# Attention scores of 18 tiles by matmuls over the full array with zeros in the moving rows, and one weight piece held behind its step

## The chip, the cores and the metric

The kernel runs as one program on one core of a Trainium2 chip. The metric is the device time of one launch in microseconds (us); lower is better. TensorE (PE, with its weight loads listed apart as PEld), VectorE (DVE), ScalarE (ACT) and GpSimd (POOL) each work through a queue of their own; SyncE (SP) issues most of the DMAs.

## The reference

Three layers follow each other, on 4 sequences of 768 tokens with 8 heads of 48 values (384 per token):

```python
# 1. linear attention with a decaying state, for each sequence and head
for t in range(768):
    cur = einsum('bhd,bhe->bhde', u * k_t, v_t)
    y[t] = einsum('bhd,bhde->bhe', r_t, state + cur)
    state = w * state + einsum('bhd,bhe->bhde', k_t, v_t)
# 2. x = y as [3072, 384];  h = x @ w_in (2048 wide);  x2 = (h - tanh(h)) @ w_out
# 3. top-1 mixture of 8 experts: the router normalizes x2 and the expert embeddings, divides by tau;
#    out[token] = gate * (relu(x2 @ w1[e]) @ w2[e])
```

## The kernel before

The 3072 tokens are 24 tiles of 128 (`NTILE`), three tiles to a block of 384 (`TOK`), eight blocks. A tile is one chunk of one sequence, and the chunks of a sequence are four tiles apart, so that the state of a sequence is handed on from tile n to tile n + 4.

**Attention of one tile** (class `Att`, tiles 6 to 23 by `attn_tile`). The transposed r and k of a tile (`RT`, `KT`) lie in 112 rows: four pairs of heads `q` along the columns, and within a pair the head g = 0 in rows 0 to 47 and g = 1 in rows 64 to 111, with zeros between. `decay_r` and `decay_k` multiply them in place by tables of decays (`tab_r`, `tab_k`) on POOL; `bonus`, `sums` and `diagonal` make the matrices `am`, which hold the u-term on their diagonal (POOL, DVE, POOL). `scores` (L423) makes for each pair q and head g the product of 128 keys by 128 queries: eight matmuls of 48 rows, those of g = 0 in the upper half of TensorE's rows and those of g = 1 in the lower half, into two PSUM banks `pa`. `causal` (L428) copies the scores under the diagonal into `am` on DVE. `values` (L454) multiplies `am` with v and the state with `RT` into `py`, in four column groups; `state` (L475, L484, L491) brings the state forward; `result` writes the sum into `xt` as a high and a low part. Each tile of `am` comes from a ring of four buffers, two for each tile of tokens.

**The first feed-forward layer** has 16 steps for each block. In step i `ffn1` (L557) makes 9 matmuls over 384 columns into `ph`; `squares` and `small_tanh` turn `ph` into a high part `ghi` (ACT, L625) and a low part `glo` (DVE, L635); `ffn2` (L572) uses those of three steps earlier (`LAG`) in 9 matmuls into three accumulators `acc`. While a block from 2 on goes through its steps, the attention of the block after it is emitted between them, three tiles in the first 12 steps.

**The experts.** In the last block (j = 7) the weights of the first expert are loaded in four pieces, in steps 8, 9, 13 and 15 (`load_expert`): a DMA brings a piece into one of two staging buffers `eraw` (so piece 2 waits until piece 0 is converted), ACT writes its high part in two halves (L885), and DVE and POOL write the low part of one half each (L886). The last piece stands under `tc.issue_after(mark["ghi"])`, which queues what it issues on ACT behind the latest `ghi`. The staging buffers then take pieces of the second expert.

**The order.** The start-up is ordered by hand. From there on a planner places every instruction into its engine's queue by modelled times and dependencies; the engines then work through their queues in order. A buffer that is written again makes the writer wait for its last readers.

Of the kernel before, what the change touches and what calls it, by code (L numbers as in the profile page):

```python
# [8 lines left out]
F32 = mybir.dt.float32  # L9
# [5 lines left out]
ALU = mybir.AluOpType  # L15
# [14 lines left out]
def rwkv__then__tanh_ffn__then__top1_moe_kernel(  # L30
# [14 lines left out]
    nc = tc.nc  # L45
    B = 4
    H, D = w.shape
# [3 lines left out]
    E, _, FF = w1.shape  # L51
    P = 128
    HP = H // 2
    NCH = S // P
    NK = DM // P
    TB = 3
# [15 lines left out]
    PW = 112  # L72
# [25 lines left out]
    work = ctx.enter_context(tc.tile_pool(name="work", bufs=2))  # L98
    dram = ctx.enter_context(tc.tile_pool(name="dram", bufs=1, space=DRAM))
    ps = ctx.enter_context(tc.tile_pool(name="ps", bufs=8, space=PSUM))  # L100
# [18 lines left out]
    def win(i, f, n=1):  # L119
        t = wq[i][f // 4].rearrange("p (f k d) -> p f k d", k=NK, d=P)  # L120
        return t[:, f % 4:f % 4 + n] if n > 1 else t[:, f % 4]
# [37 lines left out]
    ident = const.tile([P, P], F32, name="ident")  # L159
# [10 lines left out]
    cmask = const.tile([P, P], mybir.dt.uint8, name="cmask")  # L170
# [13 lines left out]
    tab_r = work.tile([PW, HP, P], F32, name="tab_r", bufs=1)  # L184
# [34 lines left out]
    mark = {}  # L219
# [62 lines left out]
    class Logits:  # L282


        def __init__(self, c, f):
            self.c, self.f = c, f
# [51 lines left out]
    def group(kk, g):  # L338
        return divmod((kk * P + 32 * g) // 32, 3)

    class Att:


# [51 lines left out]
        def sums(self):  # L395
            self.cd = work.tile([P, HP, 2], F32, name="cd")
            nc.vector.tensor_reduce(out=self.cd.rearrange("p a b -> p (a b)"), in_=self.rk, op=ALU.add, axis=AX.X)  # L397

        def diagonal(self, on_act=False, between=None):
            self.am = []  # L400
            for g in range(2):
                a = work.tile([P, HP, P], F32, name="am", bufs=4)
                if on_act:
                    for q in range(HP):
                        ins = nc.scalar.activation(out=a[:, q, :], in_=ident, func=AF.Copy,
                                                   scale=self.cd[:, q, g:g + 1]).ins
                    if between and g == 0:
                        with tc.issue_after(ins):
                            between()
                else:  # L410
                    nc.gpsimd.tensor_tensor(out=a, in0=ident[:, None, :].to_broadcast([P, HP, P]),  # L411
                                            in1=self.cd[:, :, g:g + 1].to_broadcast([P, HP, P]), op=ALU.mult)
                self.am.append(a)

        def scores(self, qs, idle=0):

            if qs[0] == 0:
                self.pa = [ps.tile([P, HP, P], F32, tag="p", name=f"pa{g}") for g in range(2)]
                fill(self.pa[0][:, :NK, :], idle)
            for q in qs:  # L420
                for g in range(2):
                    o = 64 * g
                    nc.tensor.matmul(out=self.pa[g][:, q, :], lhsT=self.KT[o:o + D, q, :], rhs=self.RT[o:o + D, q, :],  # L423
                                     start=True, stop=True)

        def causal(self):
            for g in range(2):
                nc.vector.copy_predicated(out=self.am[g], mask=cmask[:, None, :].to_broadcast([P, HP, P]),  # L428
                                          data=self.pa[g])
# [68 lines left out]
    def attn_tile(n):  # L498
        t = Att(n, None)
        with ExitStack() as es:  # L500
            for x in fence.pop(n, ()):
                es.enter_context(tc.issue_after(x))
            t.decay_r(nc.gpsimd)
            t.decay_k(nc.gpsimd)
            t.bonus(nc.gpsimd)
            t.sums()
            t.diagonal()
            t.decayed()
        yield
        t.scores(range(HP))  # L510
        t.causal()
        yield
        yield
        yield

        j = n // TB
        if j not in xts:
            xts[j] = work.tile([P, NK, 2, TOK], F32R, name="xt")
        t.xt = xts[j]
        t.values()  # L520
        t.state()
        t.result()
        yield
        yield
# [7 lines left out]
    def store_x(j, xt):  # L532
        with tc.issue_after(mark["w"]):
            nc.sync.dma_start(out=blocks(xd, j * TOK).rearrange("(p a) d -> p (a d)", p=P),
                              in_=xt.rearrange("p k i t -> p (k i t)").bitcast(F32))

    def attention(j):
        for n in range(TB * j, TB * j + TB):
            if 2 * TB + 1 < n + 1 < NTILE:
                load_rkv(n + 1)  # L540
            yield from attn_tile(n)


    def fill(bank, n):

        for _ in range(n):
            nc.tensor.matmul(out=bank, lhsT=ones16, rhs=ones16[:, None, :].to_broadcast([P, NK, P]), start=True,
                             stop=True)

    def ffn1(lhs, rhs, nk, n, idle=0, by_part=False):  # L550

        ph = ps.tile([P, n], F32, tag="p", name="ph")
        fill(ph, idle)
        turns = [(kk, p) for kk in range(nk) for p in range(3)]
        for kk, p in sorted(turns, key=lambda x: x[1]) if by_part else turns:
            a, b = ((0, 0), (0, 1), (1, 0))[p]
            mark["ph"] = nc.tensor.matmul(out=ph, lhsT=lhs[a][:, kk, :], rhs=rhs(b, kk),  # L557
                                          start=(kk == 0 and p == 0), stop=(kk == nk - 1 and p == 2)).ins
        return ph

    def columns_of(xt):
        return lambda p, kk: xt[:, kk, p, :]
# [46 lines left out]
    def squares(ph, between=None):  # L609
        z = work.tile([P, TOK], F32, name="z")  # L610
        q = work.tile([P, TOK], F32, name="q")
        nc.scalar.activation(out=z, in_=ph, func=AF.Square)  # L612
        if between:
            between()
        nc.scalar.activation(out=q, in_=z, func=AF.Square, scale=SS, bias=sb_t)  # L615
        return z, q

    def small_tanh(ph, parts, step, between=iter(())):

        z, q = parts  # L620
        ghi = work.tile([P, TOK], F32R, name="ghi", bufs=LAG + 1)
        glo = work.tile([P, TOK], F32R, name="glo", bufs=LAG + 1)
        nc.vector.tensor_tensor(out=ph, in0=ph, in1=z, op=ALU.mult)  # L623
        nc.vector.scalar_tensor_tensor(out=ph, in0=q, scalar=KC, in1=ph, op0=ALU.add, op1=ALU.mult)  # L624
        mark["ghi"] = nc.scalar.activation(out=ghi, in_=ph, func=AF.Copy).ins  # L625

        def outliers():
            mk = work.tile([P, TOK], BF16, name="mk", bufs=1)
            nc.scalar.activation(out=mk, in_=z, func=AF.Relu, bias=lz_t, accum_out=zx[:, step:step + 1])  # L629

        if step >= 2:
            outliers()
            for _ in range(3):
                next(between, None)
        mark["glo"] = nc.vector.tensor_tensor(out=glo, in0=ph, in1=ghi.bitcast(F32), op=ALU.subtract).ins  # L635
        if step < 2:
            late.append(outliers)
        return ghi, glo
# [807 lines left out]
    at = (-1, -1) + CONV  # L1446
    turns = {at[order.index(2 * c + 1)] + 1: c for c in range(NF // 2)}
    for i in range(len(steps) + 1):
        if i < len(steps):
            j, f = steps[i]  # L1450
# [85 lines left out]
    for j in (0, *range(2, NB)):  # L1536
        xt = xts.pop(j)
        store_x(j, xt)
        att = attention(j + 1) if 0 < j < NB - 1 else third
        na = 0 if j > 0 else 4  # L1540
        for n, i in enumerate(range(*spans[j])):
            ph = ffn1([win(p, i) for p in range(2)], columns_of(xt), NK, TOK)
            pend.append((j, i, small_tanh(ph, squares(ph), j * NF + i)))
            while na < ((n + 1) * 18 // NATT if j > 0 else 5 + 3 * n // 2):
                next(att, None)
                na += 1
            if len(pend) > LAG:
                ffn2_next()
            if n in FIN.get(j, FIN[NB]):
                next(fin, None)  # L1550
            if n in LIST.get(j, LIST[NB]):
                lists.pop(0)()
            if j == NB - 1 and i == 8:
                for _ in fin:
                    pass
                lists.pop(0)()
                order_first()
                places(0, 0, TB)
                sl = rows(0, 0, TB)
                gate = {}  # L1560
                ld = load_expert(0, sxi[0:1, 0, 1:2], gate, (nc.vector, nc.gpsimd))
                wides[0] = wide(0, sl)
            if j == NB - 1 and i in (8, 9, 13, 15):
                with tc.issue_after(mark["ghi"]) if i == 15 else ExitStack():
                    next(ld, None)
            if j == NB - 1 and i in COL0:
                next(wides[0])
        for _ in att:
            pass
# [92 lines left out]
```

## Time and profile before

| | us |
|---|---|
| runs | 769.98, 771.24, 769.98 (median 769.98) |
| the profiled execution | 771.22, of which the span of its instructions is 769.6 |
| PE busy | 756.2 (98% of the span), 6143 matmul records |
| PEld, DVE, ACT, POOL busy | 718.4, 464.8, 457.1, 300.5 |

A busy share says how much of the span an engine had work in hand; matmuls overlap in a pipeline, so what a matmul costs is read from the distance between starts, not from its own duration. A matmul of plain float32 operands stands in the trace as two records, one of `float32r` or bfloat16 as one.

### The profile page before, as it was taken

Reading aid. Unit: us, or ns where it says so; the run is one execution under the profiler, and the core shown is the slowest. Engines: PE = TensorE matmul, PEld = TensorE weight load, DVE = VectorE, ACT = ScalarE, POOL = GpSimd, SP = SyncE. Lnnn points to the kernel's source line nnn. Section 1 sums busy time; section 2 is a strip of 40 time slices with the busy share of each in tenths; the row PEclk is TensorE's granted clock in tenths of the full one; section 3 lists DMA queues with packets and bytes.
Section 4 is the critical chain, followed back from the end, with each engine's and each line's share of the span. In section 5 each row is a group of like instructions: output and inputs, shape, how many; then the busy total and the mean of one; then the engine's idle time right before and its main releaser. Section 6 shows DMA issues by size and latency. Waiting matters only on the chain.

```text
span 769.6 us, 15995 instructions
## 1 busy us (share of the span) xinstructions
PE 756.2 (98%) x6143; PEld 718.4 (93%) x6143; DVE 464.8 (60%) x1037; ACT 457.1 (59%) x1064; POOL 300.5 (39%) x362
## 2 busy tenths in 40 slices
PE   9899999999999999999999999999999999999996
PEld 5689899999999999999999999999989999999996
DVE  7967976667656565565555655656684455545430
ACT  5787676655657556656657756768463535544431
POOL 3743680466781671753564341133530202110111
PEclk9899999999999999999999999999999999999999
DMA  8964355243240330232223101052374435454400
GB/s 263 288 206 142 118 170 200 64 165 100 66 148 24 126 122 2 91 94 87 80 69 123 59 32 64 14 171 85 116 229 143 129 115 189 150 173 161 154 31 32
DMA packets 41016, 92.21 MB, mean 120 GB/s; under 512 B 4827, under 2 KB 20597, under 8 KB 39907
## 3 DMA queue, kind: packets, MB, share of 16 engines
q1 hardware_dynamic: 36274, 81.44, 33.0%
q0 software_dynamic: 4240, 9.67, 3.5%
q8 instruction: 50, 0.82, 0.4%
q14 instruction: 36, 0.29, 0.1%
q10 hardware_dynamic: 416, 0.00, 0.0%
HBM read 67.26 MB, written 24.00 MB: 119 GB/s over the span
## 4 chain that ended last, share of the span: by engine, by line
PE 90%; issue 3%; DVE 3%; ACT 2%; DMA 2%; POOL 1%; POOLq 0%; SPq 0%; DVEq 0%; ACTq 0%
PE acc L572 39%; PE ph L557 37%; PE py L454 5%; PE pa L423 3%; DMA eraw<-in_moe_w_dram 2%; PE pt L908 1%; PE warm L158 1%; PE pst L475 1%; POOL out_dram L827 0%; PE pt L293 0%; DVE bits L267 0%; DVE wraw L270 0%; PE pl L303 0%; DVE bits L264 0%; PE accn L1036 0%
## 5 line engine op out<-in xcount | busy, mean ns | idle before, releaser
L557 PE MATMUL ph<-xt,wq 128*128 128x384 f32 (+4 forms) x1712 | 340.1, 341 | 1.9 <-ACT wt L295 1.3
L557 PEld LDWEIGHTS ph<-xt,wq 128*128 128x128 f32 x1712 | 302.7, 188 | 5.9 <-ACT wt L295 1.5
L572 PE MATMUL acc<-wq,ghi 128*128 128x392 f32 (+2 forms) x1120 | 289.1, 343 | 0.9 <-ACT ghi L625 0.9
L572 PEld LDWEIGHTS acc<-wq,ghi 128*128 128x128 f32 (+1 forms) x1120 | 200.3, 187 | 5.9 <-ACT ghi L625 1.2
L572 PE MATMUL acc<-wq,glo 128*128 128x392 f32 (+2 forms) x552 | 182.2, 340 | 0.1
L612 ACT ACTIVATE z<-ph 128x384 f32<-128x384 f32 x128 | 62.8, 490 | 105.0 <-PE ph L557 104.7
L623 DVE TENSOR_TENSOR ph<-ph,z 128x384 f32<-128x384 f32 x128 | 72.0, 563 | 62.6 <-ACT z L612 62.0
L572 PEld LDWEIGHTS acc<-wq,glo 128*128 128x128 f32 (+1 forms) x552 | 102.7, 187 | 0.9 <-DVE glo L635 0.7
L635 DVE TENSOR_TENSOR glo<-ph,ghi 128x384 fp32r<-128x384 f32 x128 | 70.7, 553 | 45.7 <-ACT ghi L625 45.6
L827 POOL DMA_INDIRECT out_dram<-ob,gts x27 | 27.2, 1008 | 176.6 <-ACT ob L917 171.4
L625 ACT ACTIVATE ghi<-ph 128x384 fp32r<-128x384 f32 x128 | 62.6, 490 | 41.0 <-DVE ph L624 37.6
L615 ACT ACTIVATE q<-z,sb_t 128x384 f32<-128x384 f32 x128 | 78.9, 617 | 3.4
L624 DVE SCALAR_TENSOR_TENSOR ph<-q,ph 128x384 f32<-128x384 f32 x128 | 71.7, 560 | 12.5 <-ACT q L615 3.5
L629 ACT ACTIVATE mk<-z,lz_t 128x384 bf16<-128x384 f32 x128 | 77.1, 603 | 0.0
L653 DVE SCALAR_TENSOR_TENSOR glo<-ph,ghi 128x384 fp32r<-128x384 f32 (+2 forms) x56 | 30.7, 549 | 63.8 <-ACT ghi L651 63.8
L651 ACT ACTIVATE ghi<-ph 128x384 fp32r<-128x384 f32 (+4 forms) x56 | 27.5, 491 | 67.6 <-PE ph L557 67.5
L411 POOL TENSOR_TENSOR am<-ident,cd 128x512 f32<-128x512 f32 x36 | 36.8, 1045 | 77.8 <-DVE cd L397 77.1
L886 DVE TENSOR_TENSOR wq<-eraw,wq 128x768 fp32r<-128x768 f32 x60 | 55.1, 955 | 11.5 <-ACT wq L885 11.0
L885 ACT ACTIVATE wq<-eraw 128x768 fp32r<-128x768 f32 x64 | 50.4, 839 | 6.2 <-DMA eraw<-in_moe_w_dram 6.2
L278 POOL TENSOR_TENSOR wq<-wraw,wq 128x768 fp32r<-128x768 f32 (+1 forms) x17 | 30.3, 1782 | 39.6 <-ACT wq L277 38.5
L716 POOL DMA_INDIRECT tab<-tk,irow x24 | 24.4, 1019 | 31.8 <-DVE tk L744 25.1
L491 POOL TENSOR_TENSOR st<-st,pw 112x384 f32<-112x384 f32 x20 | 16.7, 840 | 49.2 <-DVE st L484 43.7
(287 smaller groups left out, 860.0 us busy)
## 6 DMA issues: line engine op xcount, KB each, us to landing
eraw<-in_moe_w_dram SPq DMA_DIRECT2D x32, 768.0 KB, 4.5
rkv<-in_rows_dram SPq DMA_DIRECT2D x18, 640.0 KB, 5.6
tt<-in_cols_dram SPq DMA_DIRECT2D x22, 448.0 KB, 4.4
xd<-xt SPq DMA_DIRECT2D x8, 1152.0 KB, 8.0
wraw<-in_moe_w_in_dram SPq DMA_DIRECT2D x8, 768.0 KB, 8.6
wraw<-in_moe_w_out_dram SPq DMA_DIRECT2D x8, 768.0 KB, 5.2
rkv<-xe SPq DMA_DIRECT2D x22, 192.0 KB, 4.4
xe<-zero SPq DMA_DIRECT2D x2, 1536.0 KB, 15.4
```

Source lines behind the costliest of these rows:

```text
L454: nc.tensor.matmul(out=self.py[32 * g:32 * g + 32, kk, :], lhsT=lhs, rhs=rhs, start=start, stop=stop)
L557: mark["ph"] = nc.tensor.matmul(out=ph, lhsT=lhs[a][:, kk, :], rhs=rhs(b, kk), start=(kk == 0 and p == 0), stop=(kk == nk - 1 and p == 2)).ins
L572: mm = nc.tensor.matmul(out=acc[t][:lhs.shape[1]], lhsT=lhs, rhs=rhs(b, i), start=(i == span[0] and p == 0), stop=(i == span[1] - 1 and p ...
L612: nc.scalar.activation(out=z, in_=ph, func=AF.Square)
L615: nc.scalar.activation(out=q, in_=z, func=AF.Square, scale=SS, bias=sb_t)
L623: nc.vector.tensor_tensor(out=ph, in0=ph, in1=z, op=ALU.mult)
L624: nc.vector.scalar_tensor_tensor(out=ph, in0=q, scalar=KC, in1=ph, op0=ALU.add, op1=ALU.mult)
L625: mark["ghi"] = nc.scalar.activation(out=ghi, in_=ph, func=AF.Copy).ins
L629: nc.scalar.activation(out=mk, in_=z, func=AF.Relu, bias=lz_t, accum_out=zx[:, step:step + 1])
L635: mark["glo"] = nc.vector.tensor_tensor(out=glo, in0=ph, in1=ghi.bitcast(F32), op=ALU.subtract).ins
L885: nc.scalar.activation(out=hi[c][:, a], in_=t[:, a], func=AF.Copy)
L886: engs[s % len(engs)].tensor_tensor(out=lo[c][:, a], in0=t[:, a], in1=hi[c][:, a].bitcast(F32), op=ALU.subtract)
```

## The change

From tile 6 on, a method `masked` runs first in a tile: four DVE multiplications, each of 48 rows by two pairs of 128 columns, write r times its decay table into two tiles `rtm`, in which a pair q has 256 columns: the first 128 hold head g = 0 in rows 0 to 47, the last 128 hold head g = 1 in rows 64 to 111, and all other rows are zero from one memset at the beginning. `scores` then makes four matmuls of 112 rows by 256 columns, one for each pair, in place of eight of 48 rows by 128 columns. `RT` itself is still multiplied by the table on POOL, for `values`. The scores and the diagonals are grouped by pairs of heads instead of by row half, and `mixed`, which takes the place of `am`, is one pair of tiles for all 18 tiles, as `rtm` is: the ring of four `am` buffers is taken by these four for good.

In the last block, piece 2 of the first expert's weights (step 13) is put behind its step's `ghi` on ACT, as piece 3 already was.

```diff
@@ in the kernel's body
+    fixed = []
+
+    class Pairs:
+        def __init__(self, tiles, g):
+            self.tiles, self.g = tiles, g
+
+        def __getitem__(self, at):
+            return self.tiles[at[1] // 2][:, at[1] % 2, self.g, :]
@@ class Att
+        def masked(self, eng):
+            if not fixed:
+                fixed.extend(work.tile([P, 2, 2, P], F32, name="am", bufs=4) for _ in range(4))
+                for x in fixed[2:]:
+                    nc.gpsimd.memset(x, 0.0)
+            self.mixed, self.rtm = fixed[:2], fixed[2:]
+            for i in range(2):
+                for g in range(2):
+                    o = slice(64 * g, 64 * g + D)
+                    eng.tensor_tensor(out=self.rtm[i][o, :, g, :], in0=self.RT[o, 2 * i:2 * i + 2],
+                                      in1=tab_r[o, 2 * i:2 * i + 2], op=ALU.mult)
+
         def diagonal(self, on_act=False, between=None):
+            if self.n >= 2 * TB:
+                self.am = [Pairs(self.mixed, g) for g in range(2)]
+                for i in range(2):
+                    nc.gpsimd.tensor_tensor(out=self.mixed[i].rearrange("p q g t -> p (q g) t"),
+                                            in0=ident[:, None, :].to_broadcast([P, 4, P]),
+                                            in1=self.cd[:, 2 * i:2 * i + 2, :].rearrange("p q g -> p (q g)")[:, :, None]
+                                            .to_broadcast([P, 4, P]), op=ALU.mult)
+                return
@@ scores
+            if self.n >= 2 * TB:
+                self.pa = [ps.tile([P, 2, 2, P], F32, tag="p", name=f"pa{i}") for i in range(2)]
+                for q in qs:
+                    nc.tensor.matmul(out=self.pa[q // 2][:, q % 2], lhsT=self.KT[:, q, :], rhs=self.rtm[q // 2][:PW, q % 2],
+                                     start=True, stop=True)
+                return
@@ causal
+            if self.n >= 2 * TB:
+                for i in range(2):
+                    nc.vector.copy_predicated(out=self.mixed[i].rearrange("p q g t -> p (q g) t"),
+                                              mask=cmask[:, None, :].to_broadcast([P, HP, P]),
+                                              data=self.pa[i].rearrange("p q g t -> p (q g) t"))
+                return
@@ attn_tile
+            t.masked(nc.vector)
             t.decay_r(nc.gpsimd)
@@ steps of the last block
-                with tc.issue_after(mark["ghi"]) if i == 15 else ExitStack():
+                with tc.issue_after(mark["ghi"]) if i >= 13 else ExitStack():
                     next(ld, None)
```

## Rows read from the trace of the kernel before

**Rows 1.** The page: busy time, and the chain that ended last, by engine.

```profile
PE 756.2 (98%) x6143; PEld 718.4 (93%) x6143; DVE 464.8 (60%) x1037; ACT 457.1 (59%) x1064; POOL 300.5 (39%) x362
...
PE 90%; issue 3%; DVE 3%; ACT 2%; DMA 2%; POOL 1%; POOLq 0%; SPq 0%; DVEq 0%; ACTq 0%
```

**Rows 2.** Waits of PE: us in total, times, longest.

```profile
PE acc L572 <- ACT ghi L625: 0.9, 1, 0.9
```

**Rows 3.** Timeline of PE, two steps: start, us, instruction, count, idle before.

```profile
451.23 1.75 PE L557 MATMUL ph<-xt,wq 128*128 128x384 f32 x9
...
454.44 1.75 PE L557 MATMUL ph<-xt,wq 128*128 128x384 f32 x9
456.12 1.16 PE L423 MATMUL pa<-tt 48*128 48x128 f32 x16
...
458.94 1.75 PE L557 MATMUL ph<-xt,wq 128*128 128x384 f32 x9
```

**Rows 4.** Groups of PE by shape, 120 to 470 us: busy us, mean ns, idle.

```profile
L423 PE MATMUL pa<-tt 48*128 48x128 f32 x288 | 20.9, 285 | 0.0
L475 PE MATMUL pst<-rkv,ktok 128*16 128x48 f32 x224 | 7.2, 206 | 0.0
L454 PE MATMUL py<-am,rkv 128*32 128x128 f32 x576 | 27.1, 272 | 0.0
```

**Rows 5.** Timeline of PE around 135 us, one state product.

```profile
134.94 0.52 PE L475 MATMUL pst<-rkv,ktok 128*32 128x48 f32 x32
```

**Rows 6.** Timeline of PE around 527 us, transposes over the whole array.

```profile
526.77 1.14 PE L908 MATMUL pt<-ident,rkv 128*128 128x128 f32 x9
527.67 0.60 PE L572 MATMUL acc<-wq,ghi 128*128 128x392 f32 x2
528.12 0.34 PE L572 MATMUL acc<-wq,glo 128*128 128x392 f32 x1
```

**Rows 7.** Groups of DVE by shape, 520 to 640 us: busy us, mean ns, idle.

```profile
L912 DVE TENSOR_TENSOR xt<-pt,xt 128x256 fp32r<-128x256 f32 x6 | 2.5, 417 | 1.5 <-ACT xt L910 1.5
```

**Rows 8.** Windows, one block: us, busy of PE, PEld, DVE, ACT, POOL, then granted clock.

```profile
244.00:306.00 62.00, 62.00 (x612) 59.76 (x611) 37.16 (x83) 38.56 (x96) 32.73 (x37) 1.00 0.25 84
```

**Rows 9.** Timeline of POOL: diagonals of tile 8, decay of r of tile 9.

```profile
147.04 2.05 POOL L411 TENSOR_TENSOR am<-ident,cd 128x512 f32<-128x512 f32 x2 [2.11 <-DVE cd L397]
...
156.52 1.29 POOL L355 TENSOR_TENSOR tt<-tt,tab_r 112x512 f32<-112x512 f32 x1 [1.24 <-DMA tt<-in_cols_dram]
```

**Rows 10.** Timeline of PE: state product of tile 7, scores of tiles 8 and 9.

```profile
152.25 0.52 PE L475 MATMUL pst<-rkv,ktok 128*32 128x48 f32 x32
...
156.96 1.16 PE L423 MATMUL pa<-tt 48*128 48x128 f32 x16
...
176.42 1.16 PE L423 MATMUL pa<-tt 48*128 48x128 f32 x16
```

**Rows 11.** Timeline of DVE: the causal copies of tile 8.

```profile
158.73 1.37 DVE L428 COPY_PREDICATED am<-cmask,pa 128x512 f32<-128x512 uint8 x2
```

**Rows 12.** Timeline of ACT in the last block, 520 to 555 us.

```profile
520.23 0.84 ACT L885 ACTIVATE wq<-eraw 128x768 fp32r<-128x768 f32 x1 [1.08 <-DMA eraw<-in_moe_w_dram]
520.98 0.47 ACT L625 ACTIVATE ghi<-ph 128x384 fp32r<-128x384 f32 x1
...
522.46 0.83 ACT L885 ACTIVATE wq<-eraw 128x768 fp32r<-128x768 f32 x1
...
532.75 0.49 ACT L625 ACTIVATE ghi<-ph 128x384 fp32r<-128x384 f32 x1 [0.39 <-DVE ph L624]
...
554.21 1.57 ACT L885 ACTIVATE wq<-eraw 128x768 fp32r<-128x768 f32 x2
```

**Rows 13.** Timeline of PE in the last block, steps 12 and 13.

```profile
518.85 1.75 PE L557 MATMUL ph<-xt,wq 128*128 128x384 f32 x9
521.51 0.98 PE L572 MATMUL acc<-wq,ghi 128*128 128x392 f32 x4 [0.91 <-ACT ghi L625]
...
523.58 1.74 PE L557 MATMUL ph<-xt,wq 128*128 128x384 f32 x9
```

**Rows 14.** Timeline of SP: loads of the second expert's first two pieces.

```profile
525.26 14.48 SPq L859 DMA_DIRECT2D eraw<-in_moe_w_dram  x2
```

## The prediction

> **What bounds the kernel now.** I read the page first, then the waits of PE, then PE's timeline step by step. The page shows PE busy for 98% of the span and 90% of the chain that ended last on PE [rows 1]. A busy PE is not proof that it sets the time, so the waits come next: once the start-up is over, the only entry of any size in which PE waits for another engine is one wait of 0.9 us for a high part in the last block [rows 2]. The timeline then shows what a step costs. One without attention goes from one start of `ph` to the next in 454.44 − 451.23 = 3.21 us; the following one, with the scores of a tile in it, in 458.94 − 454.44 = 4.50 us [rows 3]. So the scores of a tile cost 1.29 us of PE's queue, and with PE as the bound every such microsecond stands in the total. In a block with attention DVE is busy for 37 of 62 us, ACT for 39 and POOL for 33, at a granted clock of 1.00, TensorE's upper level of 2.4 GHz [rows 8]. What the change does to those three counts only where it makes PE wait.
>
> **The scores, before.** A tile's eight matmuls are 16 records of 128 columns; the 18 tiles make the 288 records of the group, busy for 20.9 us, 1.16 us a tile as in the one shown [rows 3, 4]. The price of 1.29 us holds two things. The records run in pairs, upper and lower half of the rows side by side, and stream for 8 times the price of 128 columns. That price is about 0.109 us: nine transposes of 128 columns over the whole array take 1.14 us, the last one's own 0.27 us left out, for eight distances [rows 6]. So some 0.87 us are streaming, and 0.42 us are lost around it, going into the halves and out of them. Such a loss does not belong to plain float32 over the whole array: from the first of those transposes to the third `acc` matmul behind them are 1.35 us, which nine distances of 0.109 and two of the usual 0.18 us (3.21 us over 18 matmuls) fill, 1.34 us [rows 3, 6].
>
> The Trainium skill says the same of the cause: the page TensorEngine Tiling (Array Packing), section Key Properties, has it that a change of the tiling mode drains TensorE. If that drain were all that changes, the 18 tiles would win 18 × 0.42 = 7.6 us; the trace agrees on the drain, but not on the rest of the sum.
>
> **The scores, after.** There are eight records of 256 columns a tile, one after the other. What does a record's column cost? The records of 48 columns last 206 ns, those of 128 columns 272 ns: 66 ns for 80 columns, 0.825 ns a column, two cycles of 2.4 GHz [rows 4]. Ends are modelled in these records, so I want a distance as well: the state product puts 32 records of 48 columns, four side by side, into 0.52 us, so (0.52 − 0.21) / 7 = 0.044 us for each four, against 0.109 us for 128 columns, with weights of only 16 and 32 columns [rows 5, 6]. It is the moving columns that set the pace, not the loading of weights. A record of 256 columns then costs between 256 × 0.825 = 0.211 us and twice 0.109 = 0.218 us. I take 0.215: eight make 1.72 us. The zeros are streamed at full price. A tile costs 1.72 − 1.29 = 0.43 us more, 18 tiles **7.7 us** (bounds 18 × 0.40 = 7.2 and 18 × 0.45 = 8.1).
>
> **The new DVE work.** Four multiplications of 256 elements a row: a DVE operation of that size took 417 ns, so 1.67 us a tile and 30 us in all [rows 7]. In the block of the windows it raises DVE by 5 us, to 42 of 62 us [rows 8]; a `glo` is used three steps, 9.6 us, after its `ph`. I take nothing, with all 1.67 us of each tile as the bound from above, which would ask for every one of them to lie ahead of something that PE awaits. The two memsets on POOL happen once.
>
> **The shared tiles.** With one pair `rtm` for all tiles, `masked` of tile 9 can only write once the scores of tile 8 have read, at 158.1 us; it must stand before the in-place decay of r, which POOL now starts at 156.52 us [rows 9, 10]. That decay moves back to about 160 us, and with it what is queued behind it on POOL (the bonus, the diagonals, the keys' decay if the planner leaves it there). Its first readers, the scores of tile 9, come at 176.42 us [rows 10], so 16 us cover it. With one pair `mixed`, the diagonals of tile 8 (147.04 us) can't be written before the values of tile 7 are done, about 152.3 us, when the state product has begun [rows 9, 10]. They would end at 154.4 us, 4.3 us before the causal copies of tile 8 at 158.73 us [rows 11]. Nothing here reaches PE, if the planner, which knows these dependencies, queues them so. If the cover were gone, the causal copies and then the values would be late. Grouping the diagonals and the causal copies by pairs changes neither their number nor their size.
>
> **The weight piece.** Steps 12 and 13 start 523.58 − 518.85 = 4.73 us apart instead of 3.21: 1.52 us lost, 0.91 us of it as one idle stretch that `ghi` ended [rows 13]. The cause stands on ACT: it waited 1.08 us for the DMA of piece 2, converted half of it (0.84 us), and only then came to the `ghi` that PE wanted, at 520.98 us; the second half stands at 522.46 us [rows 12]. The `ghi` of step 13 is four such parts later. With the piece behind it, ACT has 1.08 us of waiting and 1.67 us of copies less in front of PE's need, more than the 1.52 us. They return as 1.67 us on ACT in steps 13 and 14, where ACT had caught up: it stood idle for 0.39 us before a `ghi` at 532.75 us, and would be there up to 2.75 us earlier [rows 12]. Two things queue behind: the low parts on DVE and POOL, needed by the first expert's second product after the block, and the load of the second expert's first piece on SP, which issued at 525.26 us as the staging buffer came free, and would move to about 530 us; its conversion is at 554.21 us [rows 12, 14]. I take **−1.5 us**; the bounds are 0 (the wait comes back with another instruction) and −1.8 (0.2 us more in the step before).
>
> **The sum.** 771.22 us of the profiled execution + 7.7 − 1.5 = 777.4 us. The median of the runs, 769.98, lies 1.24 us under that execution, so the time should be 776.2 us. By the bounds, 775.4 to 778.1.
>
> **The rivals.**
> 1. *Faster: the halves' drain was the price, and wide records are cheap.* If a record's pace were set by loading its 128 columns of weights, 0.109 us, 256 moving columns would hide behind it: 8 × 0.109 = 0.87 us, 0.42 us less a tile, 7.6 us in all, 769.98 − 7.6 − 1.5 = 760.9 us. It decides once a record of 256 columns takes under 1.29 / 8 = 0.161 us. For it speaks that 128 columns of weights and 128 moving columns are equally dear in the transposes; against it the pace of the 48-column records, whose weights are short and whose cost still goes with the moving columns [rows 4, 5]. 7%.
> 2. *The shared tiles or the new DVE work make PE wait.* A chain from values through diagonals and causal copies to the next values, tile by tile, has 4.3 us to spare where I looked; if the planner spends it, or DVE's 1.67 us stand before a `causal` that PE awaits, 0.2 to 0.4 us a tile give 3.6 to 7.2 us more: 779.8 to 783.4 us. PE's row of waits speaks against it [rows 2]. 10%.
> 3. *The piece's wait only moves.* Then only the scores count: 777.7 us. 10%.
> 4. *The wide scores pay the drain too,* 0.42 us a tile: 783.8 us. The transposes speak against it [rows 6]. 2%.
> 5. *The planner, whose whole order is made anew, gives the 6 us back by chance.* There is no idle time of PE for that beyond the stall already counted [rows 2]: 5%, about 770 us.
>
> **How the numbers follow.** The forecast has 66%, and its own range is 774.5 to 778.5 us with an order made anew. To leave out no more than two in ten, the range takes in the third rival and the lower end of the second: 773.5 to 781 us. About 0.2%, 1.5 us, is what a measurement tells from no change. Slower: the forecast and rivals 2 to 4, 88%; the same: rival 5, 5%; faster: rival 1, 7%.
>
> **What would show it.** Right: eight records of 112 rows by 256 columns a tile, about 0.215 us apart and some 380 ns long, steps with scores at about 4.9 us instead of 4.50, no lengthened matmuls at either end; PE without the wait for `ghi` near 521 us, the copies of piece 2 behind the `ghi` of step 13. Wrong: records 0.11 us apart, or waits of PE for `am`, `pa` or `glo` in the blocks with attention, or DVE standing before `masked` while a `ph` waits.

## The result, and the profile after

| | before | after |
|---|---|---|
| median of the runs, us | 770.44 (769.98 to 771.24, 4 runs) | 782.23 (780.48 to 782.94, 4 runs) |
| the profiled execution, us | 771.22 | 782.94, span 781.3 |

The ratio is 1.0149 (95% interval 1.0129 to 1.0168): 11.8 us slower. The forecast was 776.2 us with a range of 773.5 to 781.0. The sign was right, the forecast change of +6.2 us is little more than half of the measured one, and the time lies 1.2 us above the range.

Where the 11.8 us stand is read by laying the two timelines of PE over each other: the start of the same `ph` in both kernels, after less before. Each flat stretch costs nothing, each rise is a loss at a known place. (Below, steps are counted through all blocks: in before step 12 starts at 93.07 us, step 24 at 138.68, step 40 at 204.44, the experts at 538.93.)

| stretch (time in after) | the shift of `ph` goes from, to | us | what lies in it |
|---|---|---|---|
| to 93 us | 0 to 0.26 | +0.26 | the start-up |
| 93 to 145 us | 0.26 to 6.04 | +5.78 | the scores of one tile (0.44) and **5.34 of something else** |
| 145 to 481 us | 6.04 to 13.58 | +7.54 | the scores of 17 tiles, 0.44 each |
| 519 to 551 us | 13.58 to 11.78 | −1.80 | the weight piece |

Two of the three terms came as forecast; a third, of 5.3 us at one place, was not in the sum. First the forecast ones. This is the timeline of PE in after, the two steps that answer to [rows 3]:

```profile
464.36 1.75 PE L602 MATMUL ph<-xt,wq 128*128 128x384 f32 x9
...
467.58 1.75 PE L602 MATMUL ph<-xt,wq 128*128 128x384 f32 x9
469.16 1.89 PE L452 MATMUL pa<-am,tt 112*128 112x256 f32 x8
...
472.52 1.75 PE L602 MATMUL ph<-xt,wq 128*128 128x384 f32 x9
```

The step without scores takes 467.58 − 464.36 = 3.22 us as before, the step with them 472.52 − 467.58 = 4.94 us instead of 4.50: +0.44 us. The group of these records by their tile (count, then shortest, median and longest duration in ns) shows their length:

```profile
L452 PE MATMUL pa<-am,tt x144: 377/379/382, 128.7 to 470.7; 112*128 112x256 f32 x144
```

All 144 last within 5 ns of each other, none is lengthened at an end, and what the step has over one without scores, 4.94 − 3.22 = 1.72 us, is eight times 0.215 us with nothing left over. So nothing is lost around the wide records, and the zeros are streamed at full price.

The weight piece is seen on ACT and on PE in the last block of after, where [rows 12] and [rows 13] were read before:

```profile
539.73 0.48 ACT L670 ACTIVATE ghi<-ph 128x384 fp32r<-128x384 f32 x1
540.10 1.58 ACT L930 ACTIVATE wq<-eraw 128x768 fp32r<-128x768 f32 x2
```

```profile
528.99 1.75 PE L602 MATMUL ph<-xt,wq 128*128 128x384 f32 x9
...
532.17 1.75 PE L602 MATMUL ph<-xt,wq 128*128 128x384 f32 x9
...
535.37 1.39 PE L602 MATMUL ph<-xt,wq 128*128 128x384 f32 x7
```

Both halves of piece 2 now stand behind the step's `ghi`, and the steps that were 4.73 us apart are 535.37 − 532.17 = 3.20 us apart.

Now the 5.3 us. The waits of PE in after (us in total, times, longest) begin with an entry that before does not have; the `ghi` entry is a wait of 0.55 us at 120.5 us, no longer the one of the last block:

```profile
PE pt L293 <- DVE wq L313: 2.7, 1, 2.7
...
PE acc L617 <- ACT ghi L670: 0.6, 1, 0.6
```

In the timeline of PE that wait, in brackets, stands at 97 us. The later `ph` and transposes behind it are slow:

```profile
96.70 0.34 PE L617 MATMUL acc<-wq,glo 128*128 128x392 f32 x1
99.74 0.62 PE L293 MATMUL pt<-ident,wraw 128*128 128x128 f32 x3 [2.71 <-DVE wq L313]
100.12 1.97 PE L617 MATMUL acc<-wq,ghi 128*128 128x392 f32 x6
101.88 0.84 PE L293 MATMUL pt<-ident,wraw 128*128 128x128 f32 x3
102.38 2.54 PE L602 MATMUL ph<-xt,wq 128*128 128x384 f32 x9
104.75 0.69 PE L617 MATMUL acc<-wq,glo 128*128 128x392 f32 x3
```

PE waits for a conversion on DVE (`wq`, L313, 0.17 us long). Why that came late shows in the timeline of DVE; the conversion is the last line. First the same instruction in before, then the timeline of after:

```profile
93.50 0.16 DVE L313 TENSOR_TENSOR wq<-pw__1363,wq 128x16 fp32r<-128x16 f32 x1
```

```profile
89.72 0.42 DVE L267 SCALAR_TENSOR_TENSOR bits<-wraw,bits 128x256 int32<-128x256 int32 x1
90.22 5.16 DVE L420 TENSOR_TENSOR am<-tt,tab_r 48x256 f32<-48x256 f32 x2
95.41 0.69 DVE L264 TENSOR_SCALAR bits<-wraw 128x512 int32<-128x512 int32 x1
96.01 0.56 DVE L668 TENSOR_TENSOR ph<-ph,z 128x384 f32<-128x384 f32 x1
96.60 0.90 DVE L420 TENSOR_TENSOR am<-tt,tab_r 48x256 f32<-48x256 f32 x1
...
97.86 0.42 DVE L420 TENSOR_TENSOR am<-tt,tab_r 48x256 f32<-48x256 f32 x1
...
99.51 0.17 DVE L313 TENSOR_TENSOR wq<-pw__1363,wq 128x16 fp32r<-128x16 f32 x1
```

L420 is the new `masked` (its tiles `rtm` bear the name `am` in the trace). Two of its operations together take 5.16 us: the first the usual 0.42 us, the second, from 90.66 us on, **4.72 us**. The timeline of POOL over the same stretch gives the reason:

```profile
89.66 0.99 POOL L415 MEMSET am<- 128x512 f32 x2
90.62 1.29 POOL L369 TENSOR_TENSOR tt<-tt,tab_k 112x512 f32<-112x512 f32 x1
91.87 1.01 POOL L403 TENSOR_TENSOR rk<-rkv 128x384 f32<-128x384 f32 x1
92.83 1.01 POOL L399 TENSOR_TENSOR ktok<-rkv,ktab 128x384 f32<-128x384 f32 x1
93.81 1.28 POOL L369 TENSOR_TENSOR tt<-tt,tab_k 112x512 f32<-112x512 f32 x1
95.05 1.20 POOL L399 TENSOR_TENSOR ktok<-rkv,ktab 128x384 f32<-128x384 f32 x1
96.22 1.00 POOL L404 TENSOR_TENSOR rk<-rk,u_bc 128x384 f32<-128x384 f32 x1
```

From 90.62 us on POOL runs operation after operation with no gap. The DVE operation that was started beside it ends at 95.38 us, 0.29 us after the fourth of them; the one of 0.90 us that starts at 96.60 us ends at 97.50 us, 0.28 us after the operation that POOL had in hand. The first one, of 0.42 us, ran beside a memset, which reads nothing.

The stall costs twice. These are windows of after (length, busy time of PE, PEld, DVE, ACT and POOL with counts, then the granted clock):

```profile
92.00:96.00 4.00, 4.00 (x26) 4.00 (x25) 3.97 (x2) 0.36 (x3) 4.00 (x4) 1.00 0.00 0
96.00:100.00 4.00, 1.29 (x8) 0.97 (x7) 3.87 (x10) 1.76 (x4) 2.86 (x4) 1.00 0.00 0
100.00:104.00 4.00, 4.00 (x17) 3.89 (x17) 4.00 (x11) 3.11 (x8) 2.27 (x2) 0.57 0.00 0
104.00:108.00 4.00, 4.00 (x32) 3.54 (x31) 3.39 (x8) 2.63 (x7) 4.00 (x4) 1.00 0.00 0
```

PE had no idle time from 84 to 97 us, stood for 2.71 us, and then the granted clock fell to its lower level, 1.2 GHz, from about 100.5 to 103.9 us (0.50 in finer windows), before it came back. From the first transpose at 99.74 us to the `acc` at 104.75 us are 5.01 us; a kernel of the experiments below (POOL waits) does the same 21 matmuls, with no stall before them, in 3.35 us. So: 2.86 us of standing (3.04 us between two starts less the usual 0.18), 1.66 us of slow clock and entry, 0.55 us of the wait at 120.5 us. That is 5.07 of the 5.34 us; 0.3 us I cannot place.

### The profile page after: what moved, and what is told of

The parts are those of the page before. It is cut to its first block, busy times and chain, and to the rows that moved or that the text cites. A ratio compares the mean times of both kernels' runs of the same rounds, so it can differ in the third digit from the quotient of the medians.

```text
span 781.3 us, 15760 instructions
## 1 busy us (share of the span) xinstructions
PE 765.2 (98%) x5999; PEld 730.9 (94%) x5999; DVE 510.2 (65%) x1109; ACT 456.6 (58%) x1064; POOL 303.8 (39%) x364
## 4 chain that ended last, share of the span: by engine, by line
PE 89%; issue 4%; DVE 3%; ACT 2%; POOL 1%; DMA 0%; POOLq 0%; SPq 0%; DVEq 0%; ACTq 0%
PE acc L617 38%; PE ph L602 37%; PE py L498 5%; PE pa L452 4%; PE pt L953 1%; PE pst L519 1%; DVE am L420 1%; PE pt L293 1%; POOL out_dram L872 0%; DVE bits L264 0%; PE pa L461 0%; PE ph L592 0%; DVE bits L267 0%; DVE wraw L270 0%; PE accn L1081 0%
## 5 line engine op out<-in xcount | busy, mean ns | idle before, releaser
L366 POOL TENSOR_TENSOR tt<-tt,tab_r 112x512 f32<-112x512 f32 x18 | 23.2, 1291 | 85.1 <-DVE am L420 85.0
L420 DVE TENSOR_TENSOR am<-tt,tab_r 48x256 f32<-48x256 f32 x72 | 41.5, 577 | 0.6
```

Of the source, the lines that this page charges most:

```text
L420: eng.tensor_tensor(out=self.rtm[i][o, :, g, :], in0=self.RT[o, 2 * i:2 * i + 2], in1=tab_r[o, 2 * i:2 * i + 2], op=ALU.mult)
```

## The experiments

The theory: one operation of `masked`, which reads two operands and writes its result in SBUF, stands while POOL works, and in DVE's densest stretch that makes PE wait. The rivals for the 5.3 us: the new layout of scores, diagonals and causal copies by pairs; the shared tiles, which move POOL's work; and the order, which the planner makes anew.

**The piece alone,** on the kernel before.

```diff
-                with tc.issue_after(mark["ghi"]) if i == 15 else ExitStack():
+                with tc.issue_after(mark["ghi"]) if i >= 13 else ExitStack():
```

> The kernel before with the weight piece's order alone. First theory (the changed kernel's time is +8.0 us of wide scores, +5.3 us lost in the steps around 90 to 125 us, -1.8 us of the piece): 770.4 - 1.8 = 768.6 us, with PE's wait for ghi near 521 us gone. Rival (the piece gains only in the order that the whole change got): 770.4 us within 0.5, with that wait or another in its place.

769.08 us (768.26 to 770.05, 11 runs) against 770.41 for before, ratio 0.9981 (0.9972 to 0.9990): −1.3 us, and the shift of `ph` goes by −1.5 us over the last block. The wait for `ghi` of [rows 2] is gone. It is faster than both kernels.

**Row halves, from the new tiles.** The change with eight matmuls of 48 rows by 128 columns again, which read `rtm`; `masked`, the shared tiles and the piece stay, the grouping by pairs goes.

```diff
-                    nc.tensor.matmul(out=self.pa[q // 2][:, q % 2], lhsT=self.KT[:, q, :], rhs=self.rtm[q // 2][:PW, q % 2],
-                                     start=True, stop=True)
+                    for g in range(2):
+                        o = 64 * g
+                        nc.tensor.matmul(out=self.pa[g][:, q, :], lhsT=self.KT[o:o + D, q, :],
+                                         rhs=self.rtm[q // 2][o:o + D, q % 2, g, :], start=True, stop=True)
```

> The changed kernel with its masked multiplications, its shared tiles and its piece order, but with the scores again as eight matmuls of 48 rows by 128 columns, read from the new tiles. First theory: the scores cost 8.0 us less, the loss around 90 to 125 us stays, 782.2 - 8.0 = 774.2 us, with a masked operation of several us near 90 us and PE's wait of 2 to 3 us near 97 us. Rival (that loss came with the planner's costs for the wide scores): 768.6 to 770 us, no such wait.

776.47 us (775.59 to 777.71), ratio 1.0075 (1.0058 to 1.0093). The price per tile is gone: the shift is flat from step 40 on to the last block. The early loss is still there (5.3 us from step 12 to step 19), so neither wide scores nor the grouping cause it. The operation at 90.27 us lasts 4.74 us. The time is above the expectation because two losses of about 1.3 us have come in. One is in tile 6's scores: its records stand in two groups of eight, one record every 0.11 us, where before has one group of 16, two at a time, in the same 1.16 us. The timeline of PE:

```profile
128.33 1.16 PE L452 MATMUL pa<-am,tt 48*128 48x128 f32 x8
...
130.68 1.16 PE L452 MATMUL pa<-am,tt 48*128 48x128 f32 x8
```

The other is a second long operation. The timeline of DVE shows it, and the waits of PE show both stalls:

```profile
201.61 4.52 DVE L420 TENSOR_TENSOR am<-tt,tab_r 48x256 f32<-48x256 f32 x1
206.16 0.56 DVE L674 TENSOR_TENSOR glo<-ph,ghi 128x384 fp32r<-128x384 f32 x1
```

```profile
PE pt L293 <- DVE wq L313: 2.7, 1, 2.7
...
PE ph L596 <- DVE glo L674: 1.1, 1, 1.1
```

Here the long operation stands ahead of a `glo`, and PE waits for it. In after there is one too, 4.45 us long at 202.53 us, with nothing urgent behind it, and PE loses nothing there: where such an operation falls decides, not how many there are.

**The new products on POOL.**

```diff
-            t.masked(nc.vector)
+            t.masked(nc.gpsimd)
```

> The changed kernel with the masked multiplications on POOL instead of DVE. First theory (a DVE operation with two SBUF inputs stands still while POOL works through operations of its own, and that stand near 90 us costs PE 5.3 us): without them on DVE the loss goes, 782.2 - 5.3 = 776.9 us, at most 2 us more where POOL's 2.7 us a tile delay it. Rival (the shared tiles or the order cost the 5.3 us): 781 us or more.

777.87 us (777.48 to 777.93), ratio 1.0096 (1.0081 to 1.0112): 7.5 us over before where the change is 11.8 over it. PE has no wait near 97 us, and the early loss is gone (shift −0.68 at step 12, −0.24 at step 24). Then come 0.44 us a tile and some 0.7 us elsewhere. It asks for 53 us of POOL, as the group of POOL shows (busy us, mean ns, idle before):

```profile
L420 POOL TENSOR_TENSOR am<-tt,tab_r 48x256 f32<-48x256 f32 x72 | 53.1, 738 | 49.3 <-PE pa L452 45.7
```

**The new scores from tile 8 on,** tiles 6 and 7 as before, so that none of the new work lies in DVE's densest stretch.

```diff
-            t.masked(nc.vector)
+            if n >= NMIX:
+                t.masked(nc.vector)
```

`NMIX` is 2 * TB + 2; `diagonal`, `scores` and `causal` ask for it too.

> The changed kernel with the new scores from tile 8 on, 16 tiles; tiles 6 and 7 as before the change. First theory (the whole loss beside the scores comes from the two tiles in the steps around 90 to 125 us; a later stand of DVE costs PE nothing): 770.4 + 16 x 0.443 - 1.8 = 775.7 us. Rival (DVE's added work costs a bit in every tile): 770.4 + 7.1 - 1.8 + 16/18 of 5.3 = 780.4 us.

776.49 us (775.79 to 777.48), ratio 1.0078 (1.0062 to 1.0093). The shift is 0.17 at step 12 and still 0.17 at step 24; then 16 tiles take it to 7.43, 0.45 each, and the piece to 5.63. The whole 5.3 us belong to the two tiles whose new work lies ahead of step 24. (Of the 5.7 us that this is nearer to before than the change, 0.9 are the two tiles' scores.)

**One input instead of two.**

```diff
-                    eng.tensor_tensor(out=self.rtm[i][o, :, g, :], in0=self.RT[o, 2 * i:2 * i + 2],
-                                      in1=tab_r[o, 2 * i:2 * i + 2], op=ALU.mult)
+                    eng.tensor_scalar(out=self.rtm[i][o, :, g, :], in0=self.RT[o, 2 * i:2 * i + 2],
+                                      scalar1=1.0, scalar2=None, op0=ALU.mult)
```

> The changed kernel with the masked operations on one SBUF input: a multiplication of r by 1.0 in place of the multiplication by its decay table, so the scores lack those decays. Elements, places and dependencies stay. First theory (an operation with two SBUF inputs stands while POOL works on operands of its own): none of the 72 operations lasts over 0.5 us, and the loss around 90 to 125 us goes: 776.9 us within 1.5. Rival (DVE's amount of work in these steps): the loss stays, 781 us or more, with operations near 0.4 us each. A third way (an operation with one input of this kind stands too): operations of over 1 us, 781 us or more.

Without the decays the main part is followed by a fallback path for general inputs, so the whole time, 6201.6 us, tells nothing, and only the trace of the main part is read. The operations by their line, and a window of the same place:

```profile
L420 DVE TENSOR_SCALAR am<-tt x72: 258/291/4477, 90.0 to 455.6; 48x256 f32<-48x256 f32 x72
```

```profile
100.00:104.00 4.00, 4.00 (x25) 3.97 (x24) 4.00 (x11) 3.69 (x9) 2.23 (x2) 1.00 0.00 0
```

The operation is quicker when nothing is beside it (291 ns against 422), but the one at 90.56 us still lasts 4.48 us, through the same four operations of POOL. So my words "two operands" in the theory fall: this form with one input stands as well. PE waited 2.36 us here, and the granted clock stayed at 1.00; the shift at step 24 is 3.32, of which 0.44 are the tile's and 2.9 the stall's. That this is 2.4 us under the 5.3 of the change agrees with the 1.66 us of slow clock and the 0.55 us of the second wait, both absent here.

**POOL waits.** The change, but in tiles 6 and 7 two tiny copies on POOL read `rtm`, and that tile's POOL work is queued behind them. DVE does exactly the new work of the change; POOL just isn't beside it.

```diff
+            if n < 2 * TB + 2:
+                jk = work.tile([P, 2, 2], F32, name="jk", tag="ix")
+                for i in range(2):
+                    m = nc.gpsimd.tensor_copy(out=jk[:, i], in_=t.rtm[i][:, 1, :, P - 1])
+                es.enter_context(tc.issue_after(m.ins))
```

> The changed kernel, in which POOL reads the masked tiles of tiles 6 and 7 by two tiny copies before it begins with that tile's own work, so that POOL stands idle while DVE multiplies. First theory (POOL's run holds DVE's operation): the four operations near 90 us last 0.4 us each, and of the 5.3 us at least 3.5 go: 776.9 to 778.7 us. Rival (DVE's amount of work or its place): 781 us or more.

776.88 us (776.38 to 777.48), ratio 1.0085 (1.0064 to 1.0107): 6.8 us over before, 5.0 us less than the change. The timelines of DVE and of POOL:

```profile
88.99 0.85 DVE L420 TENSOR_TENSOR am<-tt,tab_r 48x256 f32<-48x256 f32 x2
...
91.06 0.42 DVE L420 TENSOR_TENSOR am<-tt,tab_r 48x256 f32<-48x256 f32 x1
...
91.84 0.42 DVE L420 TENSOR_TENSOR am<-tt,tab_r 48x256 f32<-48x256 f32 x1
...
93.48 0.17 DVE L313 TENSOR_TENSOR wq<-pw__1363,wq 128x16 fp32r<-128x16 f32 x1
...
93.90 0.68 DVE L270 SCALAR_TENSOR_TENSOR wraw<-wraw,bits 128x512 int32<-128x512 int32 x1
```

```profile
89.99 0.19 POOL L551 COPY jk<-am 128x2 f32<-128x2 f32 x1 [0.58 <-DVE am L420]
92.39 0.19 POOL L551 COPY jk<-am 128x2 f32<-128x2 f32 x1 [2.21 <-DVE am L420]
92.53 1.29 POOL L366 TENSOR_TENSOR tt<-tt,tab_r 112x512 f32<-112x512 f32 x1
93.78 1.31 POOL L369 TENSOR_TENSOR tt<-tt,tab_k 112x512 f32<-112x512 f32 x1
```

All four take 0.42 us, the conversion starts at 93.48 us as in before, and the wait is gone. The last line of DVE is a control: L270 runs wholly beside POOL's L369 in its usual 0.68 us; its `bits` lie in PSUM. The shift goes from −0.99 at step 12 to 7.47 after the last tile, 8.46 us (18 × 0.44 = 8.0, and 0.5 at one place), and the piece gives 1.8 back.

**All pieces behind `ghi`,** on the kernel before.

```diff
-                with tc.issue_after(mark["ghi"]) if i == 15 else ExitStack():
+                with tc.issue_after(mark["ghi"]) if i >= 8 else ExitStack():
```

> The kernel before with the first two weight pieces behind their steps' high parts as well, besides piece 2. If ACT's wait of 5.1 us for the first piece's DMA costs PE the 0.25 us of the step before and no more: 769.0 us, as the piece alone, less 0.3. Rival (piece 1 frees its staging buffer later, and its conversions come into the steps that piece 2 now uses): 769.5 us or more, with PE waits for a high or low part near 525 us.

769.00 us (768.25 to 769.97, 12 runs) against 770.10 for before, ratio 0.9984 (0.9974 to 0.9994): by the medians the same as with piece 2 alone. In its trace the shift goes by −1.8 us over the last block, against −1.5 with piece 2 alone, and the 0.26 us of the step before are in it. That is the 0.3 us expected, too little for the medians to tell.

## Why the prediction was right and wrong

- **The wide scores: right.** Forecast 0.215 us a record, some 380 ns long, 0.43 us a tile, 7.7 us in all. Measured: 0.215 to 0.220 us between starts, 379 ns, 0.44 us a tile, 8.0 us. The pace worked out from the records of 48 columns [rows 4, 5] held, so the first rival (columns of weights set the pace) and the fourth (a drain) fall. The loss of 0.42 us around the row halves is really gone; the zeros cost 0.86 us in its place.
- **The shared tiles: right.** The shift rises only by the tile's price from one tile to the next in the long stretch, so the chain from values to the next tile's diagonals had its cover.
- **The weight piece: right.** Forecast −1.5 with bounds of 0 and −1.8; −1.8 in the change's trace; for the piece alone −1.5 in its trace and −1.3 by the medians. The third rival falls.
- **The new DVE work: wrong, the step that failed.** It was costed by the length of one operation, 417 ns [rows 7], and "I take nothing"; the measured cost is 5.3 us at one place. The length is right for an operation with nothing beside it (422 ns in the median). But that row reads PSUM (`pt`), while `masked` reads and writes SBUF alone, as POOL's operations do. The average load of a block from 244 us on [rows 8] also spoke for the wrong place: the first of the new work falls at 90 us, where DVE still cuts weights and is busy for 14.9 of the 16 us from 84 to 100 us in before. The 72 operations are busy for 41.5 us where 30 were counted, and one of them sets off 5.3 us. Even the bound from above was of the wrong kind: "all 1.67 us of each tile" is a sum of lengths, and a stand is no part of a length. Nor did that bound, 30 us, enter the sum: 775.4 to 778.1 holds the bounds of the scores and the piece alone.
- **The second rival** had the place (DVE's work makes PE wait) and a band that holds the result, 779.8 to 783.4 us, but by 0.2 to 0.4 us in every tile. Three experiments on this point (POOL waits, the products on POOL, new scores from tile 8 on) bring 4.3 to 5.0 us back, scores left out not counted. The first two keep the new layout and the shared tiles in every tile, so neither of these is the cause. Each of the three is ordered anew by the planner, so the order is not held fixed. But from step 12 to step 24 PE has the same records in all of them, tile 6's scores apart: 45.61 us in before, 5.78 more in after, and 0.42, 0.44 and 0.00 more in these three. With POOL waiting the sum of the prediction stands within 0.7 us: 776.9 us where 776.2 were forecast.

One row of before could have told it: the same kind of operation, r times its table, which DVE does in the start-up (shortest, median and longest in ns):

```profile
L355 DVE TENSOR_TENSOR tt<-tt,tab_r x4: 674/692/1402, 7.9 to 31.8; 112x512 f32<-112x512 f32 x4
```

The one of 1402 ns started at 31.77 us, while POOL had L358 in hand. A maximum of twice the median in a group of four is a question; I read only means.

The Trainium skill has the rule, on the page SBUF — State Buffer, section Who interferes with whom: a VectorE instruction with both inputs in SBUF contends with a GpSimd instruction that reads SBUF, not with one that only writes it; one in a two-port mode contends with GpSimd too, and of that mode it says that whichever issues first has the shared ports for the whole instruction while the other is blocked. The trace agrees in four points: two SBUF inputs stood for 4.72 us, a one-input float32 `tensor_scalar`, whose 291 ns look like such a mode, for 4.48 us, operations with an operand in PSUM kept their time (0.68 us), and a memset on POOL did no harm (0.42 us). Taken by the page's words, the price would be the one instruction of POOL in hand, 1.3 us at most; the runs show four in a row.

## What to carry to other kernels

Zeros in the moving rows are no free way around the row halves: they are streamed at the full price of their columns, here 0.86 us a tile against 0.42 us of loss around the halves. When work is added to VectorE beside GpSimd, ask first where its operands lie, since an operation from SBUF to SBUF can last as long as a run of GpSimd operations (order the two after each other where the stretch is dense, and judge the densest stretch, not an average one). A bulk conversion queued behind the small result that TensorE awaits is a cheap gain: one condition, 1.3 us.

## What the runs showed of the hardware

- An operation of DVE that stands beside POOL is let in where a POOL operation ends: those of 0.87 us and more in after, seven of 72, end 0.27 to 0.29 us after the end of one. Not at every end: at 90.66 us it took four operations (4.72 us), at 167.79 us one (0.87 us). In the five kernels that keep this work on DVE the longest lasts 4.03 to 4.74 us. What chooses the end is open; no run was made for it.
- After 2.71 us without matmuls the granted clock was at 1.2 GHz for some 3.4 us, which cost 1.66 us more (in the kernel with row halves, 2.70 us and again some 3.4 us); after 2.36 us in the one-input kernel it stayed at 2.4 GHz. A stall is thus dearer than its own length, and not in proportion.
